# Moving three x loads to another queue, a layernorm into an earlier stretch, and four half tiles into one place, in an S5 + SwiGLU kernel

## The chip, the core and the metric

The kernel runs on one core of one Trainium2 chip. TensorE (PE) does the matmuls, VectorE (DVE) the elementwise work, the scans and the layernorm statistics, ScalarE (ACT) the activations and most copies out of the matmul accumulators (PSUM, eight banks), GpSimd (POOL) a power function and the accumulating output transfers, and SyncE (SP) issues most transfers and the transposes done by DMA. Each engine works through its own instruction stream in the order in which the program emitted it, and waits on semaphores for what other engines make. The metric is the device time of one execution in microseconds (us).

## The reference, cut to what matters

`x` is 2048 rows of 512 columns in bf16. The output is `x + A(xn) + B(xn)`, with `xn` the layernorm of each row of `x`:

```python
xn = _layernorm(x)                                   # (x - mean) / sqrt(var + 1e-5)
# A: a diagonal complex state space, P = 512 states, over t = 0..2047
h  = Lam_bar * h + Bu[:, t]                          # Bu = xn @ B_bar^T
y  = 2.0 * Re(hseq @ Cmat^T) + xn * Dskip
# B: SwiGLU with F = 1376
(silu(xn @ w_gate) * (xn @ w_up)) @ w_down
```

## The kernel before, in words

The 2048 rows are 16 row tiles (`n`) of 128, and four chunks (`c`) of 512 rows (`CW`). Everything on PE works from `xnT`, the normalised rows transposed: 128 columns of D on the partitions, `KD` = 4 such blocks, rows along the free axis.

How a chunk of `xnT` comes to be. Chunk 0 is made row tile by row tile at the start (the head): `ln_stats` (DVE), `ln_rstd_act` (two small ACT operations), `norm_dve`, a transpose on PE (`xT_pe`), a copy to `xnT`. Between these, `head_mm` already does gate and up matmuls of the first three F tiles for each row tile. For chunks 1 to 3, `ln_rest` gives a list of small operations: four `ln_stats` and `fin` (variance plus epsilon on DVE, then a power on POOL), then `nbf` (the value `nb` = -mean * rstd, DVE), then four operations that normalise one row tile each and issue its transpose by DMA on SP's queue (`xT_dma`). For chunks 2 and 3 the normalising is on ACT (`norm_act`), and it needs `nb`. All chunks share one buffer `xn`.

The PE work of a chunk is: `gateup_chunk` (11 F tiles; a gate bank and an up bank each, four matmuls of 512 columns per bank; ACT then takes silu of the gate bank and copies the up bank, and DVE multiplies pairs of tiles, the `product`s), `bproj_chunk` (eight banks, copied by ACT to `u16`), and `out_chunk`: four row tiles of `out_ffn` (11 matmuls each into a bank that stays open) followed by `out_ssm` (8 more into the same bank). F = 1376 leaves a last tile of 96 columns. `gateup_last` computes its 96 gate columns and 32 of its up columns in one matmul group; the other 64 up columns (`wu_last`) are done for two chunks at once, one chunk in each half of the array's columns, in the odd chunk's `gateup_last`.

The DVE work of the state space (`ssm_ops`) per chunk is six large rotations (forward), eight scans, a small carry (six tiny operations), and six rotations back, which write `wt` for `out_ssm`.

What sets the order. Each engine's order is written out by hand. DVE operations stand in a list, `backlog`, filled by `queue` and `spread` (which puts one operation of a second list behind each of a first). After each PE piece, `pump` adds the estimated PE time to an account (`owed`) and emits operations from the list while their estimated costs are covered; `need(tag)` emits everything up to the last operation of that tag. An emitted operation brings its ACT, POOL and SP instructions with it, so ACT's order is settled by the same list. In the profile's line numbers: L183 the statistics, L202 `nb`, L207/L212 normalising on DVE/ACT, L219/L223 transpose on PE and copy, L227 transpose by DMA, L352/L354 B projection and its copy, L362 to L376 rotations, L394 scans, L403 to L408 carry, L427 gate and up, L441/L442 silu and copy, L446 product, L453 to L457 the last tile, L463/L466/L468 its 64-column halves, their copies, and its product, L514 `out_ffn`, L524 `out_ssm`, L581 the dummy matmuls ahead of the work, L609 `head_mm`.

Around chunks 1 and 2 the order before is: `bproj_chunk(1)`, `gateup_chunk(1)`, `bproj_chunk(2)`, `out_chunk(0)`, `gateup_chunk(2)`, `bproj_chunk(3)`. Chunk 2's layernorm is spread among chunk 0's scans, chunk 3's among chunk 1's scans.

Of the kernel before, what the change touches and what calls it, by code (L numbers as in the profile page):

```python
# [11 lines left out]
BF16 = mybir.dt.bfloat16  # L12
ALU = mybir.AluOpType
# [10 lines left out]
def kernel(  # L24
# [17 lines left out]
    nc = tc.nc  # L42
    _, L, D = A_x.shape
# [3 lines left out]
    CW = 512  # L47
    HW = CW // 2
    NT = L // 128
    NCH = L // CW  # L50
    TPC = CW // 128
    KD = D // 128
    NQ = Pst // 128
    FT = (F + 127) // 128
# [4 lines left out]
    LA, LB = 32, 64  # L59
# [8 lines left out]
    up_p = ctx.enter_context(tc.tile_pool(name="up_p", bufs=4))  # L68
# [5 lines left out]
    def bank(shape=(128, CW), dtype=F32):  # L74
        return psum.tile(list(shape), dtype, name="ps")
# [4 lines left out]
    x_v = A_x[0].rearrange("(n p) d -> p n d", p=128)  # L80
# [5 lines left out]
    xall = const.tile([128, NT, D], BF16, name="xall")  # L86
    xnT = const.tile([128, KD, L], BF16, name="xnT")

    fgroups = [(0, 3), (3, 7), (7, FT - 1)]
    wg_g, wu_g = [], []  # L90
# [5 lines left out]
    wu_last = const.tile([128, KD, LB], BF16, name="wu_last")  # L96
# [14 lines left out]
    def load_w1(q, tiles, view, gi):  # L111
        a, b = fgroups[gi]
        q.dma_start(out=tiles[gi][:], in_=view[:, :, a * 128:min(F, b * 128)])


    def load_w1_half(tiles, view, gi, k0, k1):
        a, b = fgroups[gi]
        nc.sync.dma_start(out=tiles[gi][:, k0:k1, :], in_=view[:, k0:k1, a * 128:min(F, b * 128)])  # L118

    nc.sync.dma_start(out=xall[:, 0, :], in_=x_v[:, 0, :])  # L120
    nc.vector.memset(xall[:, 1, 0:2], 0.0)
    nc.scalar.dma_start(out=xall[:, 1, :], in_=x_v[:, 1, :])
    nc.scalar.preload_act_table_set("natural_log_exp_and_others")
    load_w1_half(wg_g, wg_v, 0, 0, KD // 2)
    load_w1_half(wg_g, wg_v, 0, KD // 2, KD)
    nc.sync.dma_start(out=xall[:, 2, :], in_=x_v[:, 2, :])  # L126
    load_w1_half(wu_g, wu_v, 0, 0, KD // 2)
    load_w1_half(wu_g, wu_v, 0, KD // 2, KD)
    nc.sync.dma_start(out=xall[:, 3, :], in_=x_v[:, 3, :])
    load_w1(nc.sync, wg_g, wg_v, 1)  # L130
    load_w1(nc.sync, wu_g, wu_v, 1)
    prm_rows = const.tile([128, 128], BF16, name="prm_rows")
# [44 lines left out]
    def xn_tile(c):  # L177
        if c not in xn_c:
            xn_c[c] = lnp.tile([128, TPC, D], BF16, name="xn")
        return xn_c[c]  # L180

    def ln_stats(n):
        nc.vector.bn_stats(out=stats[:, n, 0, :], in_=xall[:, n, :])  # L183
        nc.vector.bn_aggr(out=mv[:, n, :], in_=stats[:, n, 0, :])
# [20 lines left out]
    def norm_dve(n, lo=0, hi=D):  # L205
        c, i = divmod(n, TPC)
        nc.vector.tensor_scalar(out=xn_tile(c)[:, i, lo:hi], in0=xall[:, n, lo:hi], scalar1=mv[:, n, 0:1],  # L207
                                scalar2=rstd[:, n:n + 1], op0=ALU.subtract, op1=ALU.mult)
# [31 lines left out]
    V = nc.vector  # L240
# [179 lines left out]
    gu_tiles = {}  # L420
    u_pair = {}
    products = []
# [7 lines left out]
    def gu_tile(c):  # L430
        if c not in gu_tiles:
            gu_tiles[c] = gut.tile([128, FT, CW], BF16, name="guT")
        return gu_tiles[c]
# [14 lines left out]
    up_last = {}  # L448

    def gateup_last(c):  # L450
        ps = bank()
        for k in range(KD):
            nc.tensor.matmul(ps[:], lhsT=w_last[:, k, :], rhs=xnT[:, k, c * CW:(c + 1) * CW],  # L453
                             start=(k == 0), stop=(k == KD - 1))
        u = up_last[c] = up_p.tile([128, CW], BF16, name="ul", bufs=2)
        nc.scalar.activation(out=gu_tile(c)[0:LB + LA, FT - 1, :], in_=ps[0:LB + LA], func=ACT.Silu)
        nc.scalar.copy(out=u[LB:LB + LA, :], in_=ps[LB + LA:128])  # L457
        if c % 2 == 0:
            return
        ps = bank()  # L460
        for k in range(KD):
            for i in range(2):
                nc.tensor.matmul(ps[i * LB:(i + 1) * LB], lhsT=wu_last[:, k, :],  # L463
                                 rhs=xnT[:, k, (c - 1 + i) * CW:(c + i) * CW], start=(k == 0), stop=(k == KD - 1))
        for i in range(2):
            nc.scalar.copy(out=up_last[c - 1 + i][0:LB, :], in_=ps[i * LB:(i + 1) * LB])  # L466
            g, u = gu_tiles[c - 1 + i][0:LB + LA, FT - 1, :], up_last[c - 1 + i][0:LB + LA, :]
            products.append(lambda g=g, u=u: V.tensor_tensor(out=g, in0=g, in1=u, op=ALU.mult))  # L468

    def gateup_tile(c, fi):  # L470
        if fi == FT - 1:
# [67 lines left out]
    def queue(tag, ops, at=None):  # L539
        ops = [[op[0], op[1], op[2] if len(op) > 2 else None, tag] for op in ops]  # L540
        if at is None:
            backlog.extend(ops)
        else:
            backlog[at:at] = ops

    def step():
        for item in backlog[0:AHEAD + 1]:
            if item[2] is not None:
                item[2]()
                item[2] = None  # L550
        cost, op, _, _ = backlog.pop(0)
        op()
        owed[0] -= cost

    def pump(us):

        owed[0] += us
        while backlog and owed[0] >= backlog[0][0] * 0.5:
            step()
        if not backlog:  # L560
            owed[0] = 0.0
# [7 lines left out]
    def need(tag):  # L569

        while any(item[3] == tag for item in backlog):
            step()
# [6 lines left out]
    def dummy(n, cols):  # L579
        for _ in range(n):  # L580
            nc.tensor.matmul(warm[:, 0:cols], lhsT=junk[:, 0:128], rhs=junk[:, 0:cols], start=True, stop=True)  # L581

    def ln_rest(c, on_act):
        ops = [(0.7, lambda n=n: ln_stats(n)) for n in range(c * TPC, (c + 1) * TPC)]
        def fin():
            ln_rstd(c * TPC, (c + 1) * TPC)
        def nbf():
            ln_nb(c * TPC, (c + 1) * TPC)
        ops += [(0.1, fin)]
        tail = [(0.1, nbf)]  # L590
        for n in range(c * TPC, (c + 1) * TPC):
            def one(n=n):
                (norm_act if on_act else norm_dve)(n)
                xT_dma(n)
            tail.append((0.05 if on_act else 0.35, one))
        return ops, tail
# [6 lines left out]
    def head_mm(i, groups, k0=0, k1=KD, tiles=range(H)):  # L603
        which = 0 if groups is wg_g else 1
        for fi in tiles:
            if len(held) <= fi:
                held.append((bank(), bank()))
            for k in range(k0, k1):
                nc.tensor.matmul(held[fi][which][:, i * 128:(i + 1) * 128], lhsT=wslice(groups, fi, k),  # L609
                                 rhs=xnT[:, k, i * 128:(i + 1) * 128], start=(k == 0), stop=(k == KD - 1))  # L610

    HK = KD // 2
    dummy(10, CW)
    ln_stats(0)
    ln_rstd_act(0)
    ln_stats(1)
# [6 lines left out]
    norm_dve(1)  # L623
    head_mm(0, wg_g, 0, HK)
    xT_pe(1)
    head_mm(0, wu_g, 0, HK)
    ln_stats(2)
    ln_rstd_act(2)
    head_mm(0, wg_g, HK, KD)
    head_mm(0, wu_g, HK, KD)  # L630
    ln_stats(3)
    norm_dve(2)
    ln_rstd_act(3)
    head_mm(1, wg_g)
    xT_pe(2)
# [25 lines left out]
    def bproj_chunk(c):  # L661
        need(f"ln{c}")
        for part in range(2):
            for q in range(NQ):
                bproj_tile(c, part, q)
                pump(BP)
                multiply(0 if q else 1)

    def gateup_chunk(c):
        for fi in [FT - 1, *range(FT - 1)]:  # L670
            gateup_tile(c, fi)
            pump(GU)
            multiply(1)

    def out_chunk(c):

        multiply(0)
        for n in range(c * TPC, (c + 1) * TPC):
            out_ffn(n)
            pump(FT * 0.2163)  # L680
        need(f"ssm{c}")
        need("cf")
        for n in range(c * TPC, (c + 1) * TPC):
            out_ssm(n)
            pump(2 * NQ * 0.2163)

    def spread(ops, others, tag, tag2):

        others = list(others)
        for op in ops:  # L690
            queue(tag, [op])
            if others:
                queue(tag2, [others.pop(0)])

    def queue_ssm(c):
        fwd, back = ssm_ops(c)
        queue(f"ssm{c}", fwd + back)
# [10 lines left out]
            multiply(0 if q else 1)  # L708
    fwd0, back0 = ssm_ops(0)
    stats2, norm2 = ln_rest(2, True)  # L710
    queue("ssm0", fwd0[0:2] + [(1.5, params_b)] + fwd0[2:6])
    queue("ln2", stats2)
    queue("ssm0", fwd0[6:8])
    spread(fwd0[8:] + back0, norm2, "ssm0", "ln2")
    queue("cf", c_ops())
    load_late()
    for fi in range(G0, FT):
# [6 lines left out]

    bproj_chunk(1)
    fwd1, back1 = ssm_ops(1)
    stats3, norm3 = ln_rest(3, True)
    queue("ssm1", fwd1[0:6])
    queue("ln3", stats3)
    queue("ssm1", fwd1[6:8])  # L730
    spread(fwd1[8:] + back1, norm3, "ssm1", "ln3")
    gateup_chunk(1)
    nc.gpsimd.dma_start(out=dsk_bc[:], in_=A_Dskip.partition_broadcast(128))
    bproj_chunk(2)
    nc.sync.dma_start(out=out[0, 0:(NT - TPC) * 128, :], in_=A_x[0, 0:(NT - TPC) * 128, :])
    queue_ssm(2)
    out_chunk(0)
    gateup_chunk(2)
    bproj_chunk(3)
    fwd3, back3 = ssm_ops(3)  # L740
    queue("ssm3", fwd3)
# [42 lines left out]
```

## Time and profile before

| | |
|---|---|
| time, median of 3 runs | 181.02 us (180.70 to 181.13) |
| the profiled execution | 181.21 us, of which the profile's span is 179.4 us |
| PE busy | 173.4 us, 97% of the span |
| DVE busy | 155.0 us, 86% |
| ACT busy | 104.8 us, 58% |
| POOL busy | 23.4 us, 13% |
| granted TensorE clock | 0.999 |

The span is what the profile sees of the program; the 1.8 us beside it lie around it. A timeline line gives the start, the length, the engine, the kernel line, the operation, output<-input, how many instructions are merged, and in brackets how long the engine had been idle and what released it. "PEld" is PE's weight load, "SPq" the queue of DMA issues on SyncE.

### The profile page before, as it was taken

The page shows a single profiled execution, that of the slowest core. Times are in us where ns is not written, and L with a number is a line of the kernel's source. Part 1 is how long each engine was busy: PE and PEld are TensorE (multiplying, and loading weights), DVE is VectorE, ACT ScalarE, POOL GpSimd, SP SyncE. Part 2 cuts the span into 40 slices and gives each one's busy share as a digit, 9 for nine tenths or more (in the row PEclk, how much of TensorE's full clock was granted, in tenths as well). Part 3 has the DMA queues.
Part 4 walks back from the last instruction along what each step waited for, and adds up shares of the span by engine and source line. Part 5 has one row for each costly group of instructions (what it writes and reads, how often), then busy time and mean ns, then how long its engine had stood idle before and what let it go on. Part 6 is the DMA issues. An engine that isn't in the chain of part 4 may idle for free.

```text
span 179.4 us, 2491 instructions
## 1 busy us (share of the span) xinstructions
PE 173.4 (97%) x908; PEld 83.4 (46%) x924; DVE 155.0 (86%) x248; ACT 104.8 (58%) x190; POOL 23.4 (13%) x30
## 2 busy tenths in 40 slices
PE   7899999999999999999999999999999999999993
PEld 2684444443444444444444444444444444444742
DVE  3649998799999999999999999999999986996033
ACT  3459956998299959022799661024866949805000
POOL 7001100000500000025400000014000004315000
PEclk9999999999999999999999999999999999999999
DMA  5999757994036600011840000007300007964512
GB/s 147 294 263 210 163 98 177 357 190 109 5 72 168 252 4 0 0 11 22 112 93 2 0 0 4 0 0 80 37 0 5 0 0 109 139 103 45 76 58 61
DMA packets 28492, 15.53 MB, mean 87 GB/s; under 512 B 18336, under 2 KB 28416, under 8 KB 28448
## 3 DMA queue, kind: packets, MB, share of 16 engines
q1 hardware_dynamic: 24592, 11.87, 28.5%
q0 software_dynamic: 3456, 3.28, 14.4%
q10 hardware_dynamic: 432, 0.23, 0.4%
q8 instruction: 7, 0.11, 0.3%
q14 instruction: 5, 0.04, 0.1%
HBM read 8.03 MB, written 5.24 MB: 74 GB/s over the span
## 4 chain that ended last, share of the span: by engine, by line
PE 93%; DMA 2%; SPq 1%; DVE 1%; issue 1%
PE ps L427 36%; PE ps L514 21%; PE ps L352 15%; PE ps L524 15%; DMA xall<-in_A_x_dram 2%; PE ps L609 2%; PE ps L453 2%; PE ps L463 1%; SPq L118 1%; DVE stats L183 0%; PE ps L219 0%; SPq L126 0%; SPq L120 0%; DVE xn L207 0%; DVE xall L527 0%
## 5 line engine op out<-in xcount | busy, mean ns | idle before, releaser
L514 PE MATMUL ps<-wd_sb,guT 128*128 128x512 bf16 (+4 forms) x195 | 38.6, 355 | 0.2
L427 PE MATMUL ps<-xnT,wg 128*128 128x512 bf16 x143 | 37.6, 379 | 0.3
L427 PE MATMUL ps<-xnT,wu 128*128 128x512 bf16 x146 | 37.5, 379 | 0.1
L394 DVE TENSOR_TENSOR_SCAN g<-r_t,car,u 128x512 bf16<-128x512 f32 x24 | 28.9, 1263 | 0.0
L524 PE MATMUL ps<-CF,wt 128*128 128x512 bf16 (+2 forms) x140 | 28.1, 355 | 0.2
L352 PE MATMUL ps<-xnT,BT 128*128 128x512 bf16 x126 | 28.2, 379 | 0.1
L514 PEld LDWEIGHTS <-guT 128*128 128x128 bf16 (+1 forms) x198 | 18.5, 98 | 19.9
L441 ACT ACTIVATE guT<-ps 128x512 bf16<-128x512 f32 x40 | 25.2, 629 | 2.5 <-PE ps L427 2.3
L442 ACT CAST u<-ps 128x512 bf16<-128x512 f32 x40 | 24.7, 618 | 2.7 <-PE ps L427 2.7
L427 PEld LDWEIGHTS <-wu 128*128 128x128 bf16 x148 | 14.5, 98 | 17.5
L427 PEld LDWEIGHTS <-wg 128*128 128x128 bf16 x148 | 14.3, 98 | 17.6 <-issue 0.8
L530 ACT CAST res<-ps 128x512 bf16<-128x512 f32 x12 | 6.8, 582 | 23.5 <-PE ps L524 23.5
L524 PEld LDWEIGHTS <-wt 128*128 128x128 bf16 x144 | 13.4, 98 | 14.3
L531 POOL DMA_DIRECT2D out_dram<-res x12 | 10.5, 1033 | 72.6 <-ACT res L530 67.5
L352 PEld LDWEIGHTS <-BT 128*128 128x128 bf16 x128 | 12.5, 98 | 15.1
L354 ACT CAST u<-ps 128x512 bf16<-128x512 f32 x32 | 17.7, 614 | 2.4 <-PE ps L352 2.2
L486 ACT ACTIVATE xr<-xall,nb,rstd 128x512 bf16<-128x512 bf16 x16 | 12.0, 808 | 8.4 <-DVE xall L492 5.9
L183 DVE BATCH_NORM_STATS2 stats<-xall 128x6 f32<-128x512 bf16 x16 | 10.7, 671 | 3.2 <-DMA xall<-in_A_x_dram 3.2
L446 DVE TENSOR_TENSOR guT<-guT,u 128x1024 bf16<-128x1024 bf16 x20 | 13.5, 679 | 0.0
L527 DVE TENSOR_TENSOR xall<-ps,xall 128x512 bf16<-128x512 f32 (+2 forms) x6 | 3.1, 514 | 9.1 <-PE ps L524 9.1
L199 POOL TENSOR_TENSOR rstd<-ve,neg_half 128x4 f32<-128x4 f32 x3 | 5.3, 1751 | 43.6 <-DVE ve L198 43.6
L362 DVE TENSOR_TENSOR pm<-u,c 128x2048 bf16<-128x2048 bf16 x8 | 9.8, 1221 | 1.2 <-ACT c L279 1.1
(101 smaller groups left out, 169.0 us busy)
## 6 DMA issues: line engine op xcount, KB each, us to landing
out_dram<-in_A_x_dram SPq DMA_DIRECT2D x1, 1536.0 KB, 8.7
out_dram<-res POOLq DMA_DIRECT2D x12, 128.0 KB, 3.2
out_dram<-xall POOLq DMA_DIRECT2D x3, 512.0 KB, 5.7
wd_sb<-in_B_w_down_dram SPq DMA_DIRECT2D x1, 1280.0 KB, 10.1
xall<-in_A_x_dram SPq DMA_DIRECT2D x1, 1024.0 KB, 5.9
wg<-in_B_w_gate_dram SPq DMA_DIRECT2D x1, 512.0 KB, 6.1
wu<-in_B_w_up_dram SPq DMA_DIRECT2D x1, 512.0 KB, 7.1
xall<-in_A_x_dram SPq DMA_DIRECT2D x1, 512.0 KB, 7.9
```

The costliest lines, as they stand in the source:

```text
L183: nc.vector.bn_stats(out=stats[:, n, 0, :], in_=xall[:, n, :])
L352: nc.tensor.matmul(ps[:], lhsT=BT[:, part, k, q * 128:(q + 1) * 128], rhs=xnT[:, k, c * CW:(c + 1) * CW], start=(k == 0), stop=(k == KD - 1))
L354: nc.scalar.copy(out=u_tiles[c][:, part, q, :], in_=ps[:])
L394: V.tensor_tensor_scan(out=g()[:, part, q, :], data0=r_t[:, q:q + 1].to_broadcast([128, CW]), data1=u_tiles[c][:, part, q, :], initial=ini ...
L427: nc.tensor.matmul(ps[:fs, lo:hi], lhsT=wslice(groups, fi, k), rhs=xnT[:, k, c * CW + lo:c * CW + hi], start=(k == 0), stop=(k == KD - 1))
L441: nc.scalar.activation(out=guT[:fs, fi, :], in_=psg[:fs], func=ACT.Silu)
L442: nc.scalar.copy(out=u_pair[c][:fs, fi % 2, :], in_=psu[:fs])
L446: products.append(lambda: V.tensor_tensor(out=g, in0=g, in1=u, op=ALU.mult))
L486: nc.scalar.activation(out=box["xr"][:], in_=xall[:, n, :], func=ACT.Identity, scale=rstd[:, n:n + 1], bias=nb[:, n:n + 1])
L514: nc.tensor.matmul(o[:], lhsT=gu_tiles[c][:fsz[fi], fi, i * 128:(i + 1) * 128], rhs=wd_sb[:fsz[fi], fi, lo:hi], start=(fi == 0), stop=False)
L524: nc.tensor.matmul(o[:], lhsT=w_tiles[c][:, part, q, i * 128:(i + 1) * 128], rhs=CF[:, part, q, lo:hi], start=False, stop=(part == 1 and q ...
L531: nc.gpsimd.dma_start(out=out_v[:, n, lo:hi], in_=res[:, lo:hi], accum_op=ALU.add)
```

## The change

Three things change. (1) Row tiles 1 to 3 of `x` are all issued from ScalarE's queue at the start; before, tile 1 was, and tiles 2 and 3 stood between weight loads on SyncE's queue. In the head one dummy matmul of ten is dropped, `norm_dve(2)` stands ahead of `ln_stats(3)`, and the first half of tile 0's up matmuls moves behind the second half of its gate matmuls. (2) Chunk 3's layernorm moves from among chunk 1's scans to among chunk 0's last scans, carry and back rotations. (3) The 64-column up halves of all four chunks are computed in one place, `up_halves`, between `gateup_chunk(1)` and `bproj_chunk(2)`, after `need("ln2")` and `need("ln3")`; their results are kept in four `ul` tiles. Chunk 2's first four F tiles go between `out_ffn` and `out_ssm` of chunk 0, and its last F tile comes last.

```diff
     nc.sync.dma_start(out=xall[:, 0, :], in_=x_v[:, 0, :])
     nc.vector.memset(xall[:, 1, 0:2], 0.0)
-    nc.scalar.dma_start(out=xall[:, 1, :], in_=x_v[:, 1, :])
+    for n in range(1, TPC):
+        nc.scalar.dma_start(out=xall[:, n, :], in_=x_v[:, n, :])
     nc.scalar.preload_act_table_set("natural_log_exp_and_others")
...
-    nc.sync.dma_start(out=xall[:, 2, :], in_=x_v[:, 2, :])
...
-    nc.sync.dma_start(out=xall[:, 3, :], in_=x_v[:, 3, :])
...
+    def up_halves():
+        pair = [bank() for _ in range(0, NCH, 2)]
+        for c0, ps in zip(range(0, NCH, 2), pair):
+            for k in range(KD):
+                for i in range(2):
+                    nc.tensor.matmul(ps[i * LB:(i + 1) * LB], lhsT=wu_last[:, k, :],
+                                     rhs=xnT[:, k, (c0 + i) * CW:(c0 + i + 1) * CW],
+                                     start=(k == 0), stop=(k == KD - 1))
+        for c0, ps in zip(range(0, NCH, 2), pair):
             for i in range(2):
...
+                nc.scalar.copy(out=last_up(c0 + i)[0:LB, :], in_=ps[i * LB:(i + 1) * LB])
+        for c in range(2):
+            last_product(c)
...
-    dummy(10, CW)
+    dummy(9, CW)
...
     xT_pe(1)
-    head_mm(0, wu_g, 0, HK)
     ln_stats(2)
     ln_rstd_act(2)
     head_mm(0, wg_g, HK, KD)
+    norm_dve(2)
+    head_mm(0, wu_g, 0, HK)
     head_mm(0, wu_g, HK, KD)
     ln_stats(3)
-    norm_dve(2)
     ln_rstd_act(3)
...
     stats2, norm2 = ln_rest(2, True)
+    stats3, norm3 = ln_rest(3, True)
     queue("ssm0", fwd0[0:2] + [(1.5, params_b)] + fwd0[2:6])
     queue("ln2", stats2)
     queue("ssm0", fwd0[6:8])
-    spread(fwd0[8:] + back0, norm2, "ssm0", "ln2")
+    spread(fwd0[8:12], norm2, "ssm0", "ln2")
+    queue("ln2", norm2[4:])
+    queue("ln3", stats3)
+    queue("ssm0", fwd0[12:14])
+    spread(fwd0[14:] + back0, norm3, "ssm0", "ln3")
     queue("cf", c_ops())
...
-    stats3, norm3 = ln_rest(3, True)
-    queue("ssm1", fwd1[0:6])
-    queue("ln3", stats3)
-    queue("ssm1", fwd1[6:8])
-    spread(fwd1[8:] + back1, norm3, "ssm1", "ln3")
+    queue("ssm1", fwd1 + back1)
     gateup_chunk(1)
     nc.gpsimd.dma_start(out=dsk_bc[:], in_=A_Dskip.partition_broadcast(128))
+    need("ln2")
+    need("ln3")
+    up_halves()
+    pump(2 * KD * 0.2163)
     bproj_chunk(2)
     nc.sync.dma_start(out=out[0, 0:(NT - TPC) * 128, :], in_=A_x[0, 0:(NT - TPC) * 128, :])
     queue_ssm(2)
-    out_chunk(0)
-    gateup_chunk(2)
+    out_chunk(0, lambda: gateup_chunk(2, range(0, 4)))
+    gateup_chunk(2, range(4, FT))
     bproj_chunk(3)
```

## The prediction, made before the changed kernel was run

> **What bounds the kernel now.** I read the busy table first, then the chain that ended last, the waits, and the timeline of the two places that the change touches.
>
> ```profile
> PE 173.4 (97%) x908; PEld 83.4 (46%) x924; DVE 155.0 (86%) x248; ACT 104.8 (58%) x190; POOL 23.4 (13%) x30
> ...
> PE 93%; DMA 2%; SPq 1%; DVE 1%; issue 1%
> ```
>
> PE is the bound: the chain is PE work from 9.31 us to 176.4. So only two things can move the time: a PE idle stretch that goes, or one that comes. The PE work itself stays the same (16 matmuls of L463 before and after; the dummy that goes lies ahead of the first real work).
>
> The largest idle stretch of PE is in the head:
>
> ```profile
> 8.04 0.69 DVE L183 BATCH_NORM_STATS2 stats<-xall 128x6 f32<-128x512 bf16 x1 [0.86 <-DMA xall<-in_A_x_dram]
> ...
> 8.87 0.38 DVE L207 TENSOR_SCALAR xn<-xall,mv,rstd 128x512 bf16<-128x512 bf16 x1
> ...
> 9.31 0.40 PE L219 MATMUL ps<-ident,xn 128*128 128x128 bf16 x4 [0.63 <-DVE xn L207]
> ```
>
> DVE waited for x tile 3, although what PE wanted was tile 2 normalised, which stood behind it.
>
> In the middle PE never waits, but DVE runs far behind the order in which its work was emitted. The place to see it is chunk 2's layernorm:
>
> ```profile
> 45.65 0.59 ACT L442 CAST u<-ps 128x512 bf16<-128x512 f32 x1 [0.27 <-PE ps L427]
> ...
> 48.08 0.40 DVE L468 TENSOR_TENSOR guT<-guT,ul 96x512 bf16<-96x512 bf16 x1
> 48.40 1.21 DVE L394 TENSOR_TENSOR_SCAN g<-r_t,u 128x512 bf16<-128x512 f32 x1
> 49.53 0.13 DVE L202 SCALAR_TENSOR_TENSOR nb<-mv,rstd 128x4 f32<-128x4 f32 x1
> ...
> 49.70 0.81 ACT L212 ACTIVATE xn<-xall,nb,rstd 128x512 bf16<-128x512 bf16 x1 [3.46 <-DVE nb L202]
> 50.42 0.58 ACT L441 ACTIVATE guT<-ps 128x512 bf16<-128x512 f32 x1
> ...
> 50.54 6.20 SPq L227 DMA_TRANSPOSE xnT<-xn  x4
> ```
>
> `nb` was emitted behind F tile 0 of chunk 1, whose matmuls end near 43.7; DVE ran it at 49.53, 5.8 us later. ACT stood for 3.46 us in front of it, with the evacuations of PE's banks queued behind. PE did not feel this, because it had eight banks to run ahead into. The transposes by DMA follow each normalised tile; the list of DMA issues says how long one takes:
>
> ```profile
> xnT<-xn SPq DMA_TRANSPOSE x12, 2.4
> ```
>
> **Part 1, the head.** Tile 2 is issued at about 1.3 us, not 2.17, tile 3 at about 1.7, not 3.68 (0.4 us of queue time each, the row of L122). ACT's table load moves from 1.31 to about 2.1 and ends at 3.4; the first ACT operation that needs it starts at 3.98, so that is hidden. Tile 2's statistics can run behind `norm_dve(1)`, which ends at 5.75: 0.88 for both instructions, ACT's two operations (behind its copy of tile 1's transposes, 6.6 to 7.2) until about 7.6, normalising until 8.0. PE comes to the transposes of tile 2 at 8.68, so the idle 0.63 goes, what was behind it now being loads that may be late: the second gate half is wanted at about 6.4, 0.8 us sooner than before, and landed at about 5.85 (issued 1.65, 4.2 us), with 256 KB of x now sharing its DMA time. The tenth dummy starts at 5.04 and holds the first transposes to 5.25; without it they start when DVE's tile is there, at about 5.1: 0.15. So 0.63 + 0.15, less a little for loads: 0.7 for PE. DVE takes part if the x of chunk 1 is there; it landed at 13.1 (issued 5.22, 7.9 us) and DVE takes it up at 13.56, so between 0.45 and 0.9. I take 0.7 for both; ends 0 (a weight half is late) and 0.9.
>
> **Part 2, chunk 3's layernorm and the halves.** `up_halves` stands directly behind the last F tile of chunk 1, and the second of its two banks multiplies chunk 3's `xnT`. So PE, which keeps its order, waits there for the fourth transpose of chunk 3, and everything is queued behind it. When does that land? DVE works without a gap here, so I add up its new order on the old clock (0.7 comes off at the end), with pitches from this timeline: scan 1.125, statistics of a tile 0.80, product 0.60, carry 0.54, `nb` 0.06, first rotations 1.13.
>
> - From 45.84, three scans: 49.22 (the product of L468, 0.32, has left this place). `nb` of chunk 2 done: 49.28.
> - Three scans 52.65; three statistics 55.05; product 55.65; the fourth and the variance 56.65; two scans 58.90; product 59.50; carry 60.04; `nb` of chunk 3 runs at 60.04 (POOL's power, 1.75 us, started at 56.6 and is done).
> - ACT starts the first tile of chunk 3 0.17 later, as at 49.70, so at 60.21. Emitted behind it: silu and copy of F tile 8, the second tile, silu and copy of F tile 9, the third and fourth tile. By the pitches at 49.70 (0.72 for a tile, 0.94 for a pair) the third starts at 63.53, the fourth at 64.25, done at 65.07.
> - SP: the third transpose is issued at 64.38, and holds the queue for 1.29 (four back to back took 5.16 at 21.95), so the fourth starts at 65.67 and lands 2.4 later: 68.07.
>
> And PE? Chunk 1 loses 0.99 of L463 here, so F tile 9 would end at 58.28 (bproj starts at 59.27 before). On the way ACT's wait in front of chunk 2's `nb` grows: ACT comes there at 45.1 and stands to 49.45, then normalises two tiles in a row. PE's eight banks from 44.4 last to 51.3; the first is freed at 51.6 and the third at 54.0, where PE wants it at 53.3: some 0.95 of PE idle. F tile 9 then ends at 59.2, the first bank of halves at 60.2, and PE stands from 60.2 to 68.1, 7.9 us.
>
> The sum: `bproj_chunk(2)` starts at 68.07 + 0.99 = 69.06 instead of 59.27, 9.8 later, and 0.99 of halves is no longer to be done in chunk 3 (125.08): +8.8. (The two idle stretches, 0.95 + 7.9, give the same.) The small wait is swallowed by the large one, since DVE alone sets when that ends.
>
> **The clock behind the stall.** The trace has no idle stretch of PE of this length but the one before the program starts. After that one the dummies' loads follow at 0.43 us:
>
> ```profile
> 2.48 0.15 PEld L581 LDWEIGHTS <-junk 128*128 128x128 bf16 x1 [0.28 <-issue]
> ...
> 2.91 0.15 PEld L581 LDWEIGHTS <-junk 128*128 128x128 bf16 x1 [0.28 <-issue]
> ```
>
> Later four matmuls of the same width take 0.865 (from 58.40 to 59.27), so 0.216 each. Nine dummies ran at half speed, 9 x 0.21 = 1.9 us lost, though the row of the granted clock shows full there. A stall of 7.9 us is nearer to that start than to a gap of 0.6, after which PE went on at full speed; so I take 1.9, ends 0 and 1.9. [...]
>
> **What moves without cost.** The copy of x to the output stands behind the transposes on SP and is issued near 67 instead of 56.8; with 8.7 us to land it is there at 76, and the first accumulating store of `out_ssm` comes after 90. Chunk 0's last product is late too (DVE 69.6), but `out_ffn` starts after 76. The coefficient work (eight times 0.7) and chunk 0's back rotations have until PE's `out_ssm` near 94, against DVE's 78. In the inserted four F tiles only four banks are free; ACT empties one in 0.48, PE fills one in 0.865. If that cover were gone it would cost PE at most 0.4 a bank, 3 us. ACT's later wait for `nb` of chunk 3 (2.76 of its 6.2 us in that row) goes, and frees nothing, as PE did not wait there. After the stall DVE is no longer behind, so PE has no new wait that I can find.
>
> Together: +8.8 - 0.7 + 1.9 = +10.0 on the profiled execution's 181.21 (span 179.4), which is 0.2 above the median: 191.2 us.
>
> **Rivals.**
> - *The clock stays full through the stall*: 189.3. For it: the granted clock reads 1.00 even over the slow dummies, so I can't see its rule. Chance 0.15.
> - *DVE is not late, only the order is*: if `nb` came in time, the fourth tile would still be emitted behind F tile 9's copy (58.9), giving tiles at 58.9 and 59.6, done 60.4, the fourth transpose issued at 61.0, landed at 63.4: +4.1, less 0.7, and 0 to 1.9 for the clock: 184.6 to 186.5. It needs DVE 5 us quicker than its rows. Chance 0.13.
> - [...] Chance 0.12.
> - *Faster*: the transposes of chunk 3 land before PE wants them, and only the head counts: 180.5. That needs the fourth tile normalised by 56.8, 2.4 us ahead of PE's 59.2; the order puts it behind a copy that can't start before 58.3. Against it stands that order itself. Chance 0.05.
>
> **How the numbers follow.** The main case has 0.55: 191.2, by itself 189.3 to 192.5 (0.4 either way for the head, 1 for the chain of ACT and SP, the clock). For 8 in 10 I take in the full clock, the upper part of the order-only case and the lower part of the larger stall: 185.8 to 193.4. A change under 0.3% (0.5 us) is about what a measurement of this kernel can't tell from none: faster 0.05, same 0.02 (a stall that just eats the head's gain), slower 0.93.
>
> **What would show it.** In the changed kernel: no idle of PE in front of tile 2's transposes near 8.5; ACT idle some 4 us in front of L211 (chunk 2) and again in front of chunk 3; PE (L474) idle for about 8 us, released by the transposes of `xnT`; matmuls 0.43 apart behind it for some 4 us; after that PE without a gap. I am wrong if `nb` of chunk 3 runs before 57, if PE waits for it less than 4 us, or if a second wait of PE of over 1 us stands later.

## The result, and the profile after

The changed kernel takes 193.02 us (median of 4 runs, 192.39 to 193.30), the kernel before 181.07 beside it: a ratio of 1.066, 95% interval 1.064 to 1.068. The forecast was 191.2 in a range of 185.8 to 193.4. The profiled execution took 193.30 us, its span is 191.5 us, 12.1 us more than that of before.

The page of the changed kernel, busy table, granted clock by slices of 4.8 us, and the shares of the chain that ended last:

```profile
PE 176.9 (92%) x907; PEld 84.6 (44%) x923; DVE 155.8 (81%) x248; ACT 106.1 (55%) x190; POOL 23.3 (12%) x30
...
PEclk9999999999999757999999999999999999999998
...
PE 66%; DVE 22%; ACT 7%; issue 2%; DMA 1%
```

PE is still the busiest engine, but the chain leaves it: 22% of the span now hangs on DVE. Every engine's busy time stayed about where it was, apart from PE's own 3.5 us more. The clock row has a hole at slices 14 to 16, which is 62 to 77 us. The timeline of PE there:

```profile
51.65 1.02 PE L426 MATMUL ps<-xnT,wg 128*128 128x512 bf16 x4 [0.42 <-ACT guT L440]
...
54.02 1.02 PE L426 MATMUL ps<-xnT,wg 128*128 128x512 bf16 x4 [0.48 <-ACT guT L440]
...
59.29 1.27 PE L474 MATMUL ps<-xnT,wu_last 128*64 128x512 bf16 x9
68.34 1.86 PE L474 MATMUL ps<-xnT,wu_last 128*64 128x512 bf16 x7 [7.78 <-DMA xnT<-xn]
70.14 9.19 PE L351 MATMUL ps<-xnT,BT 128*128 128x512 bf16 x31
79.16 9.68 PE L527 MATMUL ps<-wd_sb,guT 128*128 128x512 bf16 x44
```

PE stands 7.78 us in front of the second bank of halves, released by chunk 3's transposes. Behind it the eight B projections go from 70.14 to 79.16, 9.0 us; before they took 6.9 (59.27 to 66.17). The two short waits for banks at 51 and 54 us make 0.9 us. The windows of this stretch show the clock itself:

```profile
60.00:68.00 8.00, 0.56 (x5) 0.20 (x2) 7.93 (x12) 5.90 (x10) 0.00 (x0) 0.76 0.41 82
68.00:72.00 4.00, 3.66 (x12) 1.31 (x12) 1.84 (x4) 1.75 (x3) 0.00 (x0) 0.50 1.06 397
72.00:76.00 4.00, 4.00 (x15) 1.55 (x13) 1.50 (x2) 2.50 (x6) 0.00 (x0) 0.69 0.00 0
76.00:80.00 4.00, 3.95 (x19) 1.79 (x19) 1.64 (x3) 3.72 (x7) 0.00 (x0) 1.00 0.00 0
```

The columns are the window, busy time of PE, PE's loads, DVE, ACT and POOL, the granted clock, DMA share and GB/s. The granted clock falls to 0.50 in the idle stretch and stays there for 6.1 us of work (68.34 to 74.44). Windows of 0.1 us put the fall from 1.00 to 0.50 at 64.20, 3.6 us after PE stopped (60.56), and the return to 1.00 at 74.44.

What held the transposes back (three timelines: ACT, DVE, SP's queue):

```profile
49.60 1.52 ACT L211 ACTIVATE xn<-xall,nb,rstd 128x512 bf16<-128x512 bf16 x2 [4.65 <-DVE nb L201]
...
57.68 0.66 ACT L441 CAST u<-ps 128x512 bf16<-128x512 f32 x1
60.39 0.81 ACT L211 ACTIVATE xn<-xall,nb,rstd 128x512 bf16<-128x512 bf16 x1 [2.06 <-issue]
...
63.71 1.53 ACT L211 ACTIVATE xn<-xall,nb,rstd 128x512 bf16<-128x512 bf16 x2
```

```profile
49.42 0.14 DVE L201 SCALAR_TENSOR_TENSOR nb<-mv,rstd 128x4 f32<-128x4 f32 x1
...
60.15 0.16 DVE L201 SCALAR_TENSOR_TENSOR nb<-mv,rstd 128x4 f32<-128x4 f32 x1
```

```profile
61.23 5.84 SPq L226 DMA_TRANSPOSE xnT<-xn  x4
```

Chunk 3's `nb` comes at 60.15, and ACT starts at 60.39. The profile names no releaser there ("issue"); that ACT waited for `nb` follows from the times, and from the run below with three scans left out, where the wait is gone. ACT waited only 2.06 us: it had finished F tile 7 no sooner than 58.34. It is done with the fourth tile at 65.2, SP has issued the four transposes by 67.1, and PE goes on at 68.34.

And the head. The idle of PE ahead of tile 2's transposes is gone; another has come behind them:

```profile
9.12 0.29 ACT L193 ACTIVATE lnv<-mv,eps_t 128x1 f32<-128x1 f32 x1 [1.30 <-DVE mv L183]
...
9.45 0.20 ACT L194 ACTIVATE rstd<-lnv 128x1 f32<-128x1 f32 x1
9.56 0.57 ACT L222 COPY xnT<-ps 128x512 bf16<-128x512 bf16 x1
...
10.18 0.83 PE L622 MATMUL ps<-xnT,wg 128*128 128x128 bf16 x12 [0.67 <-ACT xnT L222]
```

ACT's copy of tile 2's transposes stands behind the two small operations of tile 3, which wait for tile 3's statistics. PE waits 0.67 us for that copy where it had waited 0.63 for the tile. The first full-width gate matmul starts at 13.08, against 13.28 before. DVE loses its part of the lead near 29 us:

```profile
29.28 0.69 DVE L273 TENSOR_SCALAR pm<-pm 128x1024 f32<-128x1024 f32 x1 [0.50 <-ACT s L278]
```

In front of this wait DVE is 0.18 us ahead of the kernel before (28.09 against 28.27). At chunk 0's first scan it is 0.22 behind (46.06 against 45.84). The wait, of 0.50 to 0.52 us, stands in the trace of every kernel with the new head and in none with the old one.

### The profile page after: what moved, and what is told of

Read it like the earlier page. It is cut to its first block, busy times and chain, and to the rows that moved or that the text cites. A ratio compares the mean times of both kernels' runs of the same rounds, so it can differ in the third digit from the quotient of the medians.

```text
span 191.5 us, 2485 instructions
## 1 busy us (share of the span) xinstructions
PE 176.9 (92%) x907; PEld 84.6 (44%) x923; DVE 155.8 (81%) x248; ACT 106.1 (55%) x190; POOL 23.3 (12%) x30
## 4 chain that ended last, share of the span: by engine, by line
PE 66%; DVE 22%; ACT 7%; issue 2%; DMA 1%
PE ps L527 20%; PE ps L426 18%; PE ps L537 14%; PE ps L351 8%; DVE stats L182 4%; DVE g L393 4%; DVE pm L361 2%; PE ps L594 2%; DVE pm L274 2%; ACT xn L211 2%; ACT u L353 2%; DMA xnT<-xn 1%; DVE mv L183 1%; DVE guT L445 1%; ACT c L278 1%
## 5 line engine op out<-in xcount | busy, mean ns | idle before, releaser
L440 ACT ACTIVATE guT<-ps 128x512 bf16<-128x512 f32 x40 | 24.4, 609 | 11.4 <-PE ps L426 11.4
L351 PE MATMUL ps<-xnT,BT 128*128 128x512 bf16 x125 | 30.2, 399 | 0.2
L441 ACT CAST u<-ps 128x512 bf16<-128x512 f32 x40 | 23.9, 599 | 4.3 <-PE ps L426 4.3
L351 PEld LDWEIGHTS <-BT 128*128 128x128 bf16 x128 | 13.0, 102 | 17.2 <-issue 3.6
L353 ACT CAST u<-ps 128x512 bf16<-128x512 f32 x32 | 17.5, 600 | 3.5 <-PE ps L351 3.4
L499 ACT ACTIVATE xr<-xall,nb,rstd 128x512 bf16<-128x512 bf16 x16 | 12.1, 809 | 8.2 <-DVE xall L505 7.6
L337 DVE SCALAR_TENSOR_TENSOR CF<-CT,nc2im,cm 128x512 bf16<-128x512 bf16 x8 | 5.8, 750 | 7.6 <-ACT cm L334 7.2
```

Source lines behind the costliest of these rows:

```text
L351: nc.tensor.matmul(ps[:], lhsT=BT[:, part, k, q * 128:(q + 1) * 128], rhs=xnT[:, k, c * CW:(c + 1) * CW], start=(k == 0), stop=(k == KD - 1))
L353: nc.scalar.copy(out=u_tiles[c][:, part, q, :], in_=ps[:])
L440: nc.scalar.activation(out=guT[:fs, fi, :], in_=psg[:fs], func=ACT.Silu)
L441: nc.scalar.copy(out=u_pair[c][:fs, fi % 2, :], in_=psu[:fs])
L499: nc.scalar.activation(out=box["xr"][:], in_=xall[:, n, :], func=ACT.Identity, scale=rstd[:, n:n + 1], bias=nb[:, n:n + 1])
```

## The experiments

Theory: the loss is PE's wait for chunk 3's transposes and the half clock behind it; the head's gain is lost to a new wait. Rivals: the moved layernorm itself, the inserted F tiles, contention as the cause of the slow matmuls, and, within the theory, which engine sets when the wait ends.

### Only chunk 3's layernorm moved

```diff
+    stats3, norm3 = ln_rest(3, True)
...
-    spread(fwd0[8:] + back0, norm2, "ssm0", "ln2")
+    spread(fwd0[8:12], norm2, "ssm0", "ln2")
+    queue("ln2", norm2[4:])
+    queue("ln3", stats3)
+    queue("ssm0", fwd0[12:14])
+    spread(fwd0[14:] + back0, norm3, "ssm0", "ln3")
...
-    spread(fwd1[8:] + back1, norm3, "ssm1", "ln3")
+    queue("ssm1", fwd1 + back1)
```

> The kernel before with chunk 3's layernorm moved among chunk 0's scans, and nothing else: the halves stay in the odd chunks, the head stays. Theory (the loss is PE's wait for chunk 3's transposes, which this kernel doesn't have there): ScalarE's wait for chunk 2's nb stays at 3.5 us with two tiles normalised in a row behind it, PE loses up to 0.9 us for want of banks: 181.1 to 182.0. Rival (the moved layernorm itself, by VectorE's and ScalarE's lateness, is most of the loss): 187 or more.

Measured: 180.85 us, ratio 1.0002 (0.9990 to 1.0015). This is less than was expected: PE has no new wait, not even the one for banks. The moved layernorm by itself costs nothing; that rival is out. The bank wait in the changed kernel goes with the 0.99 us of halves that are gone from ahead of chunk 1's F tiles there (F tile 0 starts at 40.71, here at 41.96); no run tried that alone.

### The halves of chunks 2 and 3 later

```diff
-    need("ln3")
-    up_halves()
-    pump(2 * KD * 0.2163)
+    up_halves(0, 2)
+    pump(KD * 0.2163)
...
+    def between():
+        need("ln3")
+        up_halves(2, NCH)
+        pump(KD * 0.2163)
+        gateup_chunk(2, range(0, 4))
+
-    out_chunk(0, lambda: gateup_chunk(2, range(0, 4)))
+    out_chunk(0, between)
```

> The changed kernel, but only the halves of chunks 0 and 1 at the old place; those of chunks 2 and 3 stand behind chunk 0's four out_ffn, some 16 us of PE work later, ahead of the four inserted F tiles. Theory: chunk 3's transposes have landed long before, no wait, no slow matmuls; left are 0.9 us of PE idle for want of banks and the head's 0.2: 181.6 to 182.0. Rival (the inserted F tiles with four banks open, or the new order behind them, cost PE too): 184 or more, with PE idle between 76 and 100 us.

Measured: 182.39 us, ratio 1.0091 (1.0077 to 1.0104). So 10.6 of the changed kernel's 12 us go by moving one bank of halves some 16 us later (76.69 instead of 60.2, where PE came to it). In PE's timeline the only waits left after the head are these two:

```profile
51.54 1.02 PE L426 MATMUL ps<-xnT,wg 128*128 128x512 bf16 x4 [0.43 <-ACT guT L440]
...
53.91 1.02 PE L426 MATMUL ps<-xnT,wg 128*128 128x512 bf16 x4 [0.49 <-ACT guT L440]
```

They make 0.92 us, the profiled span is 1.1 longer than the one of before. The inserted F tiles with four banks open show no wait of PE between 60 and 100 us. Against the median of before the kernel is 1.5 us slower, more than was expected; up to 0.6 us beyond the bank wait is not accounted for.

### The wait filled with dummies

```diff
+        warm2 = bank()
         for c0, ps in zip(range(0, NCH, 2), pair):
+            if c0:
+                for _ in range(32):
+                    nc.tensor.matmul(warm2[:], lhsT=junk[:, 0:128], rhs=junk[:], start=True, stop=True)
             for k in range(KD):
```

> The changed kernel with 32 dummy matmuls of 512 columns between the two banks of halves, so 6.9 us of PE work at full clock inside the 7.8 us in which PE waits for chunk 3's transposes. Theory (the slow matmuls behind the wait are the idle PE's clock): they go, bproj(2) takes 6.9 us instead of 9.0, granted clock near 1.00, 2.9 us less: 190.1. Rival (they are slow for another reason, such as the copy of x to the output that runs from 67 to 74 us): no gain, 193.0. If dummies only stood in the way: 194 or more.

Measured: 190.60 us, ratio 1.0529 (1.0508 to 1.0549), 2.4 us less than the changed kernel. PE's timeline:

```profile
60.53 7.08 PE L475 MATMUL ps<-junk 128*128 128x512 bf16 x32
67.54 0.40 PE L478 MATMUL ps<-xnT,wu_last 128*64 128x512 bf16 x1
68.58 1.02 PE L478 MATMUL ps<-xnT,wu_last 128*64 128x512 bf16 x7 [0.64 <-DMA xnT<-xn]
69.54 7.08 PE L351 MATMUL ps<-xnT,BT 128*128 128x512 bf16 x31
76.46 5.78 PE L531 MATMUL ps<-wd_sb,guT 128*128 128x512 bf16 x25
```

The transposes land no sooner (PE goes on at 68.58, 0.24 later), but the B projections take 6.9 us (69.54 to 76.46) instead of 9.0, with the same copy of x to the output beside them. The granted clock reads 1.00 in every 2 us window from 58 to 78, where the changed kernel has 0.50 from 68 to 72; the mean over the execution is 0.997 against 0.971. So the slow matmuls were the clock granted to a PE that had stood idle for 7.78 us: without the idle stretch it didn't fall here. How soon it falls was not the same in every trace: 3.6 us after PE stopped in the changed kernel (60.56 to 64.20), 2.5 us in the run with three scans left out (60.05 to 62.53).

### Three of chunk 0's scans left out

```diff
                 def scan(q=q, part=part):
+                    if c == 0 and (q, part) in ((1, 1), (2, 0), (2, 1)):
+                        nc.gpsimd.memset(g()[:, part, q, :], 0.0)
+                        return
```

> The changed kernel, with three of chunk 0's eight scans left out (their results are zeros, set by GpSimd), those between chunk 2's nb and chunk 3's statistics, so that VectorE comes to chunk 3's nb 3.4 us earlier. As the prediction had it (VectorE alone sets when the wait ends): 3.4 us less, 189.6. Theory from the trace of the changed kernel (ScalarE is behind as well, it finishes F tile 7 at 58.3 and waits for nb only 2.06 us): PE resumes 2.0 us earlier, 191.0, and ScalarE doesn't wait there any more. Rival (the place in the order alone sets it): no change, 193.0.

Measured: 190.19 us, ratio 1.0515 (1.0486 to 1.0543), 2.8 us less than the changed kernel. Time alone lies between the two sums; the timelines decide (ACT, then PE):

```profile
57.17 0.66 ACT L444 CAST u<-ps 128x512 bf16<-128x512 f32 x1
57.64 0.91 ACT L211 ACTIVATE xn<-xall,nb,rstd 128x512 bf16<-128x512 bf16 x1
```

```profile
65.69 1.86 PE L477 MATMUL ps<-xnT,wu_last 128*64 128x512 bf16 x7 [5.64 <-DMA xnT<-xn]
67.49 7.98 PE L351 MATMUL ps<-xnT,BT 128*128 128x512 bf16 x31
```

`nb` of chunk 3 ran at 56.30, 3.85 us sooner, and ACT no longer waits for it: it goes from F tile 7's copy straight to the first tile. PE's wait shrinks by 2.14 us (7.78 to 5.64), near ACT's 2.06, not by DVE's 3.4. The two profiled executions are 3.8 us of span apart (187.7 against 191.5), more than the 2.8 of the medians, and the rest of these 3.8 is clock and head: from PE's restart to the end of the B projections it is 9.6 us here (65.69 to 75.31) and 10.8 in the changed kernel, and PE stops 0.5 sooner in this execution. So VectorE alone sets the last 2 us of the wait; before that, the chain of ScalarE does. In the changed kernel ScalarE had stood 4.65 us for chunk 2's `nb` and then worked without a gap from 49.60 to 58.34. How much of the 5.64 us left is this backlog, and how much only the place in the order, was not separated.

### The head alone, and with ScalarE's order mended

The first is part 1 of the change on the kernel before. The second adds:

```diff
-    ln_rstd_act(3)
     head_mm(1, wg_g)
     xT_pe(2)
+    ln_rstd_act(3)
     norm_dve(3)
```

> The kernel before with part 1 alone: x tiles 1 to 3 from ScalarE's queue, nine dummies, tile 2 normalised ahead of tile 3's statistics. Theory: the idle 0.63 us of PE ahead of tile 2's transposes goes, but a new one of 0.67 us comes behind them, because ScalarE's copy of those transposes stands behind the two small operations of tile 3, which wait for its statistics; what is left is the dropped dummy, 0.2 us: 180.9 us, ratio 0.999. Rival (the head gives the 0.7 us of the prediction and the change loses it later): 180.4, ratio 0.996.

> As the run before, and ScalarE's two small operations of tile 3 emitted behind its copy of tile 2's transposes. If those two are what PE waited for, the 0.67 us go, less 0.2 us for tile 3's own transposes, which then come later: 180.4 us, ratio 0.9965. If the head is held by the weight loads instead, no change against the run before: 180.9.

Measured: 181.44 us, ratio 1.0039 (1.0027 to 1.0051), and 181.38 us, ratio 1.0023 (1.0010 to 1.0035). Both miss: neither is faster. The wait that the mending was meant to remove is gone (the second kernel starts its first full-width matmul at 12.40, 0.9 sooner than the kernel before). What became of the gain is seen 75 us later. The head alone, PE, ACT and DVE, and last PE in the kernel before:

```profile
10.07 0.83 PE L608 MATMUL ps<-xnT,wg 128*128 128x128 bf16 x12 [0.73 <-ACT xnT L222]
...
90.39 1.02 PE L426 MATMUL ps<-xnT,wg 128*128 128x512 bf16 x4 [0.17 <-ACT guT L440]
```

```profile
86.29 0.81 ACT L211 ACTIVATE xn<-xall,nb,rstd 128x512 bf16<-128x512 bf16 x1 [3.22 <-DVE nb L201]
```

```profile
29.20 0.69 DVE L273 TENSOR_SCALAR pm<-pm 128x1024 f32<-128x1024 f32 x1 [0.52 <-ACT s L278]
```

```profile
90.36 1.03 PE L427 MATMUL ps<-xnT,wg 128*128 128x512 bf16 x4
```

PE comes to chunk 2's B projection at 58.96 instead of 59.27, but then it runs out of banks and starts an F tile of chunk 2 at 90.39, where the kernel before starts it at 90.36. ACT stands there for chunk 3's `nb`, and DVE, which makes it, is not earlier but 0.15 later, since it now waits 0.52 us for ACT near 29 us. In the kernel before PE just made it there without a wait; a PE that is early gains nothing. Why DVE meets that wait only with the new head was not tried. This explains why the head alone gains nothing; why it is 0.56 us slower than the median of before stays open (its profiled span, 179.6, is 0.2 above the one of before). The second kernel meets the same wait (0.17 us at 89.82), but it costs only a part of the lead: PE is 0.9 us ahead at 12.40, and the last DVE addition still comes 0.55 us sooner than in the kernel before (175.87 against 176.42). That execution took 180.86 us, one of four of twelve between 180.80 and 180.97; the other eight took 181.32 to 181.48 and left no trace. So the wait at 90 us doesn't explain this kernel's median, which stays open.

### Both: the moved layernorm and the mended head

> The kernel before with chunk 3's layernorm among chunk 0's scans (as in ln3_only) and the head of head_fix. Theory: the head alone brings nothing because PE, early by 0.9 us at 59 us, waits for banks at 90 us behind chunk 3's nb, which sets the time there; with that layernorm moved away the head's 0.6 to 0.9 us reach the end: 180.0 to 180.3, ratio 0.995 to 0.997. Rival (the gain is lost elsewhere, or PE now waits for banks behind chunk 2's nb at 50 us): 180.9 or more.

Measured: 180.76 us, ratio 0.9986 (0.9974 to 0.9999). The direction is right (no wait at 90 us), the size is not. In the profiled execution the second half of the gate weights is late:

```profile
6.97 0.51 PE L608 MATMUL ps<-xnT,wg 128*128 128x128 bf16 x6 [0.35 <-DMA wg<-in_B_w_gate_dram]
```

and the first full-width matmul starts at 13.11, where the kernel before has 13.28. So x tile 3 went back to SyncE's queue, behind the four weight halves:

```diff
-    for n in range(1, TPC):
+    for n in range(1, TPC - 1):
         nc.scalar.dma_start(out=xall[:, n, :], in_=x_v[:, n, :])
...
     load_w1_half(wu_g, wu_v, 0, KD // 2, KD)
+    nc.sync.dma_start(out=xall[:, 3, :], in_=x_v[:, 3, :])
```

> As ln3_head, but x tile 3 is issued from SyncE's queue behind the four weight halves, as before, so that only tile 2 shares the transfers of the first weight halves. Theory: in the profiled run of ln3_head the second gate half was late (PE idle 0.35 us for it) and ate the head's gain; with tile 3 out of its way that wait goes: 180.1 to 180.4, ratio 0.995 to 0.997. Rival (the halves were late by the run's chance, not by tile 3): as ln3_head, ratio 0.9986; if tile 3 then comes late for its statistics, 1.000 or more.

Measured: 180.69 us, ratio 0.9979 (0.9970 to 0.9989). This is 0.2% less than the kernel before, as far as a difference of this size can be told; the 0.35 us are half of what the head gains at its own place. PE's first full-width matmul:

```profile
12.58 1.03 PE L427 MATMUL ps<-xnT,wg 128*128 128x512 bf16 x3
```

In this trace PE has no wait behind its first dummies. It is 0.7 us earlier here and 0.7 earlier at the end (last DVE addition at 175.71 against 176.42). That is against the profiled execution of before, which lay 0.2 us above its median; against the median less is left. Whether x tile 3 had made the weight half late is not settled: the intervals of this run and the one before it overlap, and the mended head without the moved layernorm, which issues x tile 3 in the same place, shows no such wait in its trace.

### The changed kernel with the head of before

> The changed kernel with the head of the kernel before. Theory: VectorE and ScalarE, not the head, set when PE goes on behind chunk 3's transposes, so the head is worth nothing here: 192.6 to 193.2. Rival (the head gives its 0.7 us): 193.7.

Measured: 191.53 us, ratio 1.0573 (1.0551 to 1.0594): outside what either theory expected, and less than the changed kernel. The profiled execution looks like the changed kernel's, with the same wait:

```profile
68.03 1.86 PE L475 MATMUL ps<-xnT,wu_last 128*64 128x512 bf16 x7 [7.78 <-DMA xnT<-xn]
```

It took 192.73 us at a mean granted clock of 0.971, like the changed kernel's four (0.970 to 0.973, 192.39 to 193.30). The other three executions of this kernel ran at 0.982 and took 191.12 to 191.90. At equal clock the new head brings nothing here, as the theory had it, and rather costs: with the old one PE goes on 0.31 us sooner (68.03 against 68.34), as `nb` of chunk 3 does (59.83 against 60.15). Most of the 1.5 us between the medians goes with the time at half clock; no trace of the three faster executions was kept, so the length of their wait is not shown. Why the changed kernel fell on the longer side in all four executions and this one in one of four is open.

## Why the prediction was right, and where its sum was off

The direction, the place and the mechanism were right, and the time was 1.8 us low (191.2 against 193.02). It lies near the upper end of the range and outside what the main case had for itself (189.3 to 192.5). PE's wait was that of the main case and no second wait came behind it; the work at half clock lasted longer. No run shows the larger stall that the range's upper end, 193.4, takes in; what the runs showed in its place is one wait of 7.78 us and 2.9 us lost at half clock. By its steps:

- *PE stands for the fourth transpose of chunk 3*: 7.9 us forecast, 7.78 measured; PE goes on at 68.34 where the sum had 68.07 less 0.7.
- *The wait for banks behind chunk 2's `nb`*: 0.95 forecast, 0.42 + 0.48 measured, at the two places named.
- *The head, -0.7*: mis-sized. The idle ahead of tile 2's transposes went, as said, but the step failed to ask what stands ahead of ACT's copy of them: tile 3's small operations, 0.67 us. PE gained 0.2. DVE, which sets the wait's end, was 0.2 later at 46 us, not 0.7 earlier, for the wait of 0.50 us at 29.28, which the step did not have. This term is 0.9 us of the miss.
- *The clock, +1.9*: mis-sized. Half clock cost 0.8 us in the second bank of halves (1.8 against 0.99) and 2.1 in the B projections, 2.9 together, over 6.1 us of work and not some 4 (68.34 to 74.44). The nearest row, the start of the program (nine dummies 0.43 us apart), was right in kind and too short. This is the other 1.0 us.
- *"DVE alone sets when that ends"*: wrong in part. ACT's chain behind the first `nb` sets it up to the last 2 us (three scans less). ACT's wait for the second `nb` was 2.06 us, not the 4 that the text gave as a sign. The time came out right because DVE's `nb` was still the later of the two.
- *What moves without cost*: behind 68.34 the changed kernel's timeline shows no wait of PE, so the four open banks, the late copy and the coefficient work were hidden as said.
- *Rivals*: the full clock was shown false by the clock row and the dummies; order alone, not lateness, would have cost 4.1 us and was not what the runs show, since taking away lateness of one engine shortened the wait. That the transposes would land in time was shown false by the 7.78 us.
- *The sum itself* was put on the profiled execution's 181.21 us, 0.2 above the median, and the 0.2 was not taken off.

## What to carry to other kernels

When work that several chunks need is gathered in one place, the place is as late as the last chunk's input, and everything behind it in that engine's order pays: PE stood 7.78 us here with chunk 2's B projections behind the halves, and one bank moved some 16 us later took 10.6 of 12 us back. Follow each input through the engines that are behind, by their own sums of durations, and check at every engine what stands ahead of the instruction on the path, not only what it waits for. And a gain at the start reaches the end only if every engine that PE meets later becomes earlier too: the trace of the head alone has PE 0.30 us ahead at 13 us and no longer ahead at 90 us, where it waits behind a DVE that came no sooner. The head showed a gain in its time, 0.2%, only together with the moved layernorm.

## What the runs showed of the hardware that was not expected

Behind PE's wait the granted clock stood at 0.50 for one of two lengths of time in the three traces, read from windows of 0.1 us. It was 10.24 us in the changed kernel (64.20 to 74.44) and in the changed kernel with the old head (63.70 to 73.94), both at a mean clock of 0.971 and with a wait of 7.78 us. It was 6.83 us with three scans left out (62.53 to 69.36), at a mean of 0.982 and with a wait of 5.64 us. The step between them is 3.41 us; 10.24 is three times that, and 6.83 twice. The fall came 3.6, 3.4 and 2.5 us after PE had stopped. The changed kernel with the old head ran at 0.971 in one execution and at 0.982 in three, 0.8 to 1.6 us faster. How long PE waited in those three is not on record, so whether the cost of a PE wait depends on more than its length was not shown. An estimate: 3.41 us less at a clock of 0.50 is worth half of that, up to 1.7 us, of PE work. What decides between the lengths no run here shows. The granted clock shows the slow matmuls in the middle of the program (0.50 from 70.0 to 74.0, weight loads of the B projection 0.43 us apart), but reads 1.00 from 1 to 5 us over the dummies at the start, which run just as slowly (loads 0.43 us apart).
